# Two attention layers on one core: the order of GpSimd's first work, and the clock that orders the instructions

## The chip, the cores and the metric

The kernel runs on one core of a Trainium2 chip. The metric is the device time of the whole program in microseconds (us). A core has a matrix engine (TensorE, PE in the profile, with its weight loads as PEld), three engines for elementwise work (VectorE or DVE, ScalarE or ACT, GpSimd or POOL), and SyncE (SP), which here only issues transfers. Transfers between memory and the core are issued by SP, ACT and POOL, each through a queue of its own, and moved by 16 DMA engines. Each engine works through its own list of instructions in the order in which the program wrote them, and waits on semaphores where it needs another engine's result.

## The reference

Two attention layers of the same size (2048 positions, width 1024, 32 heads of 32) on different inputs; their outputs stand side by side.

```python
def _A_ref(x, wqkv, wo):          # W, dil = 8, 2: each position sees itself and 7 earlier ones, every second one
    q, k, v = heads(x @ wqkv)
    logits = einsum("bhsd,bhswd->bhsw", q, k[gathered]) * scale      # masked with -1e9
    o = einsum("bhsw,bhswd->bhsd", softmax(logits), v[gathered])
    return merge(o) @ wo
def _B_ref(x, wqkv, wo):          # W = 256: each position sees itself and the 255 before it
    scores = where(mask, einsum("bhqd,bhkd->bhqk", q, k) * Dh ** -0.5, -1e9)
    o = einsum("bhqk,bhkd->bhqd", softmax(scores), v)
    return merge(o) @ wo
return concatenate([a, b], axis=-1)
```

## The kernel before, in words

**Units.** The work is cut into eight units of 512 positions: four of layer B ("dense"), then four of layer A ("dilated"; even and odd positions are separated on the host, so that a window of stride two becomes one of stride one). In each unit there are eight head groups of four heads, so 64 groups in all.

**Numbers in two parts.** Every fp32 operand of a projection is split into a high part (a rounded copy, `fp32r`) and a low part (operand minus high part); three products of parts replace one fp32 product. The split of a loaded tile is done in `Stream.parts`: a cast on ACT (L249) or DVE (L252), then one subtraction on DVE for each 512 columns (L255). So each loaded weight tile of 1024 columns costs a cast and two subtractions in a row.

**Loads.** `Stream` has one list of items (x tiles and weights) in the order of use, 512 KB each. The first six go out at once from SP and ACT, in halves where `FIRST` says so. All later ones go out from POOL (L194) into three rotating buffers; a load can start when the splits of the item three before it have read its buffer. `load_to(n)` issues loads until `n` items are loaded, and `split_to(n)` splits items and books, for the end of each split, the next call of `load_to`. The first call, at L163, asks for six items (`NRAW + len(more)`).

**Attention, dense layer.** For a group, q and k are evacuated from PSUM, split (L597, L601), and copied by SP into stacked buffers `qst` and `kst` (L621, L552 for the 256 keys of the unit before). There are two of each, used in turn. Then come 16 first scores (`s`, 96 partitions), for each of which DVE adds the mask and takes the maximum (L1356) and ACT takes the exponential and its sum (L1361); from these one row of logarithms is formed and multiplied into the stack (L1396). The second scores follow, already normalised, ACT takes the exponential into `pbuf` (L1441), and `keep` (L1417) zeroes what lies outside the window, by an affine_select on POOL (L1420) or a minimum with a mask on DVE (L1423). Two P·V matmul groups per head group follow ("o" on TensorE), each after the masks of its blocks.

**Attention, dilated layer.** Each group is copied into a seat (L580), 64 small score blocks are computed in one go, DVE runs a softmax over them (L1184 to L1214), ACT spreads the result (L1223, L1226), and P·V follows. The last eight keys of a unit are kept in `tails` for the next one (L565 reads them, L570 writes them, L568 clears them on DVE where the next unit begins a new sequence: eight times in unit 5).

**Constants.** `constants` (L452) makes masks and the identity on POOL with memsets and affine_selects (L463 to L483).

**The order.** Nothing is reordered by a compiler: the kernel is written in the order of a small simulation. `Clock` keeps a time at which each engine is free (`free`), and the main loop (L1576) takes, of four lists (auxiliary, second scores with P·V, first scores, gemm), the item that can start first by that clock; ties go to the lists in this order. An item starts on TensorE as soon as the clock thinks that what it needs is ready. `use` books an instruction on an engine, `issue` and `move` book a transfer and return when it lands, `defer` puts off work to a time of the clock, `flush` runs what is due. A choice between two engines (`parts`, `keep`, `copy_out`) compares the ends by the clock; `keep` takes POOL if it ends no more than 0.2 after DVE (`MASK_BIAS`). First scores of a dense group are held back 1.2 (`KEYS_LATE`) after the stacked copies land by the clock.

**How the clock treats shared things before the change.** POOL and a DVE instruction with two SBUF operands (`port=True`) exclude one another: POOL starts after the last such DVE instruction that has been booked, and DVE after the last POOL instruction booked. All transfers stand in one row: each takes a duration in which nothing else moves, in the first gap that holds it, and lands a tail later. `MOVE` has both numbers by kind; `LEAD` is the time from issue to the start (SP 1.34).

**The first call of `load_to`.** The loop over `FIRST` at L171 uses the name `n` for its counter, which is the name of the function's argument. After the loop `n` is 8, and the function goes on to issue items 6 and 7 from POOL, before `constants` is reached, which is run as the main loop begins. The same counter is tested against `BY_ACT` at L174.

## Time and profile before

| | us |
|---|---|
| median of 3 runs | 1803.32 |
| lowest, highest | 1802.33, 1803.51 |
| the profiled execution | 1802.41 |
| its span, first to last instruction | 1800.7 |
| mean granted TensorE clock | 0.999 |

The profile shows one execution. Its parts: busy time of each engine, the span in 40 slices, the DMA queues, the chain of work that ended last, the costliest groups of instructions, and the DMA issues. A row of the timeline has the start, the time until the end of the merged instructions, engine, line, operation, output and inputs, count, and in brackets the idle time before it with what ended it. A row of waits has who waited for whom, the total, the number of times, and the longest. A row of a group has the number of instructions, then busy time and the mean of one in ns, then idle time before them. Everything on TensorE is issued by one helper, so all its rows have the line L297, and are told apart by tiles: g for projections, s for scores, o for P·V. The chain that ended last is 87% PE:

```
PE 87%; DVE 5%; issue 3%; DMA 2%; ACT 2%; POOL 1%; DVEq 0%; POOLq 0%; ACTq 0%
```

### The profile page before, as it was taken

Reading aid. Unit: us, or ns where it says so; the run is one execution under the profiler, and the core shown is the slowest. Engines: PE = TensorE matmul, PEld = TensorE weight load, DVE = VectorE, ACT = ScalarE, POOL = GpSimd, SP = SyncE. Lnnn points to the kernel's source line nnn. Section 1 sums busy time; section 2 is a strip of 40 time slices with the busy share of each in tenths; the row PEclk is TensorE's granted clock in tenths of the full one; section 3 lists DMA queues with packets and bytes.
Section 4 is the critical chain, followed back from the end, with each engine's and each line's share of the span. In section 5 each row is a group of like instructions: output and inputs, shape, how many; then the busy total and the mean of one; then the engine's idle time right before and its main releaser. Section 6 shows DMA issues by size and latency. Waiting matters only on the chain.

```text
span 1800.7 us, 38453 instructions
## 1 busy us (share of the span) xinstructions
PE 1775.3 (99%) x14496; PEld 1439.2 (80%) x14496; DVE 1297.4 (72%) x2887; ACT 940.3 (52%) x2336; POOL 413.7 (23%) x952
## 2 busy tenths in 40 slices
PE   9999999999999999999999999999999999999999
PEld 7787777888777888778788778877888787778887
DVE  6777876768867769867678566756666768688866
ACT  4565566555656565655655444534454435355442
POOL 3222323222242222332223400110011101001120
PEclk9999999999999999999999999999999999999999
DMA  8354664644645555455546265665466558758984
GB/s 245 112 152 135 185 167 135 171 138 138 185 141 172 152 131 167 144 159 148 141 124 174 84 190 180 213 211 187 160 212 204 192 177 285 265 181 273 350 287 146
DMA packets 154794, 324.58 MB, mean 180 GB/s; under 512 B 18032, under 2 KB 58992, under 8 KB 154608
## 3 DMA queue, kind: packets, MB, share of 16 engines
q0 software_dynamic: 45792, 166.74, 29.8%
q1 hardware_dynamic: 98736, 137.02, 26.6%
q10 hardware_dynamic: 10080, 18.35, 2.7%
q8 instruction: 115, 1.88, 0.4%
q14 instruction: 71, 0.58, 0.1%
HBM read 201.33 MB, written 53.48 MB: 142 GB/s over the span
## 4 chain that ended last, share of the span: by engine, by line
PE 87%; DVE 5%; issue 3%; DMA 2%; ACT 2%; POOL 1%; DVEq 0%; POOLq 0%; ACTq 0%
PE g L297 68%; PE s L297 13%; PE o L297 6%; DMA raw<-xs 1%; DVE w L255 1%; DVE x L255 1%; ACT s L1361 0%; DVE band L1212 0%; DMA raw<-wv 0%; DVE sm L1208 0%; DVE band L1184 0%; ACT w L249 0%; DMA raw<-wqk 0%; DVE w L252 0%; DMA qst<-nat 0%
## 5 line engine op out<-in xcount | busy, mean ns | idle before, releaser
L297 PE MATMUL g<-x,w 128*128 128x512 f32 x3552 | 878.9, 393 | 5.0 <-DVE x L255 3.9
L297 PEld LDWEIGHTS g<-x,w 128*128 128x128 f32 x3552 | 654.8, 188 | 135.2 <-issue 6.6
L255 DVE TENSOR_TENSOR w<-raw,w 128x512 fp32r<-128x512 f32 x510 | 334.3, 697 | 48.5 <-ACT w L249 42.4
L1361 ACT ACTIVATE s<-s,nm 128x384 f32<-128x384 f32 (+2 forms) x512 | 274.4, 537 | 108.2 <-DVE nm L1356 101.7
L1356 DVE CUSTOM_DVE_ANT_0 s<-s,mask_d 128x384 f32<-128x384 f32 (+2 forms) x512 | 261.7, 553 | 91.7 <-PE s L297 91.4
L297 PE MATMUL g<-w,x 128*128 128x256 f32 (+1 forms) x1728 | 307.9, 327 | 2.4 <-DVE w L255 1.5
L1420 POOL TENSOR_SCALAR_AFFINE_SELECT pbuf<-pbuf 128x128 f32<-128x128 f32 (+1 forms) x603 | 218.4, 390 | 317.9 <-ACT pbuf L1441 315.9
L297 PEld LDWEIGHTS g<-w,x 128*128 128x128 f32 x1728 | 255.2, 190 | 28.0 <-DVE w L255 2.8
L297 PE MATMUL g<-r,w 128*128 128x512 f32 x960 | 239.0, 393 | 1.7 <-issue 1.2
L1441 ACT ACTIVATE pbuf<-s 128x384 f32<-128x384 f32 (+2 forms) x480 | 203.1, 505 | 64.2 <-PE s L297 62.0
L297 PEld LDWEIGHTS g<-r,w 128*128 128x128 f32 x960 | 177.2, 188 | 37.2 <-issue 2.0
L194 POOL DMA_DIRECT2D raw<-wqk x126 | 68.6, 544 | 407.4 <-DVE w L255 256.8
L297 PEld LDWEIGHTS s<-qst,kst 128*128 128x128 f32 x704 | 113.4, 188 | 42.6 <-ACT s L1361 16.8
L297 PE MATMUL s<-kst,qst 96*128 96x384 f32 (+2 forms) x512 | 142.6, 342 | 0.9 <-ACT s L1361 0.7
L297 PE MATMUL s<-qst,kst 128*128 128x256 f32 (+2 forms) x704 | 137.0, 302 | 4.0 <-ACT s L1361 3.2
L252 DVE CAST w<-raw 128x1024 fp32r<-128x1024 f32 x173 | 119.8, 692 | 19.3 <-PE g L297 9.0
L249 ACT CAST w<-raw 128x1024 fp32r<-128x1024 f32 (+1 forms) x83 | 85.8, 1038 | 71.1 <-PE g L297 29.7
L297 PEld LDWEIGHTS s<-kst,qst 96*128 96x128 f32 x512 | 93.6, 189 | 26.3 <-issue 4.4
L1361 ACT ACTIVATION_READ_ACCUMULATOR s<-s,nm 128x1 f32 x512 | 105.3, 206 | 0.0
L1223 ACT COPY wide<-band 32x512 f32<-32x512 f32 x128 | 79.0, 617 | 31.0 <-DVE band L1214 29.4
L297 PE MATMUL o<-pbuf,vbuf 128*32 128x384 f32 (+2 forms) x1408 | 91.2, 388 | 0.0
L597 ACT ACTIVATE nat<-g 128x512 fp32r<-128x512 f32 x64 | 38.3, 598 | 98.2 <-PE g L297 89.0
(90 smaller groups left out, 1432.1 us busy)
## 6 DMA issues: line engine op xcount, KB each, us to landing
raw<-wqk POOLq DMA_DIRECT2D x126, 512.0 KB, 4.6
raw<-wv POOLq DMA_DIRECT2D x60, 512.0 KB, 5.0
qst<-nat SPq DMA_DIRECT2D x96, 256.0 KB, 5.7
kst<-nat SPq DMA_DIRECT2D x96, 256.0 KB, 5.7
raw<-wo POOLq DMA_DIRECT2D x44, 512.0 KB, 4.4
raw<-xs POOLq DMA_DIRECT2D x28, 512.0 KB, 4.5
outs<-ost ACTq DMA_DIRECT2D x38, 256.0 KB, 3.1
kst<-halo SPq DMA_DIRECT2D x72, 128.0 KB, 4.5
```

The costliest lines, as they stand in the source:

```text
L194: (self.nc.scalar if early else self.nc.gpsimd).dma_start(raw if len(ap.shape) == 2 else raw.rearrange("p (a b) -> p a b", a=2), ap)
L249: nc.scalar.copy(t[:, 0, :], raw)
L252: nc.vector.tensor_copy(t[:, 0, :], raw)
L255: nc.vector.tensor_tensor(t[:, 1, c:c + 512], raw[:, c:c + 512], t[:, 0, c:c + 512].bitcast(F32), op=ALU.subtract)
L297: nc.tensor.matmul(out, left, right, **k)
L597: nc.scalar.activation(hl[:, 0, :], ps, AF.Copy, scale=sc)
L1223: nc.scalar.copy(diag[r:r + 32, :, :, c:c + 32], turned[r:r + 32, :, :, 1, :])
L1356: nc.vector.tensor_tensor_reduce(ps[:, :n], ps[:, :n], mask[:, cut:full], scale=-1.0, scalar=BIG, op0=ALU.add, op1=ALU.min, accum_out=nm)
L1361: nc.scalar.activation(ps[:, :n], ps[:, :n], AF.Exp, bias=nm, scale=-1.0, accum_out=sm)
L1420: nc.gpsimd.affine_select(w, w, pattern=[[0, m], [step, n]], compare_op=ALU.is_ge, fill=0.0, base=base, channel_multiplier=chan)
L1441: nc.scalar.activation(w, ps[:, :pack * n].rearrange("p (j n) -> p j n", j=pack), AF.Exp)
```

## The change

Four edits, in one file.

1. The counter of the loop over `FIRST` is renamed `turn`. The first call of `load_to` then ends with six items; items 6 and 7 are loaded when their buffers' splits end by the clock, which is after `constants`.
2. The clock's load is shorter with a longer tail, the sum being the same. `move` now books SP's and ACT's transfers in one row and POOL's in another; a new transfer waits for the last one of its row, and goes at half speed while one of the other row is under way. What is booked is not lengthened afterwards.
3. POOL's start in the clock is held only by the DVE instruction (with two SBUF operands) in whose booked time it falls, until that one's end. DVE still waits for the last POOL instruction booked.
4. The clearing of `tails` goes from DVE to GpSimd.

```diff
-    MOVE = dict(load=(2.12, 0.14), store=(0.64, 0.4), copy=(1.18, 0.56),
+    MOVE = dict(load=(1.5, 0.76), store=(0.64, 0.4), copy=(1.18, 0.56),
...
-        self.port = dict(dve=0.0, pool=0.0)
-        self.later, self.lands, self.busy = [], [], []
+        self.port, self.held = 0.0, []
+        self.later, self.lands, self.moves = [], [], [[], []]
...
         if eng == "pool":
-            t = max(t + 0.06, self.port["dve"])
-        elif port:
-            t = max(t, self.port["pool"])
-        return t
+            t += 0.06
+            return next((e for s, e in self.held if s <= t < e), t)
+        return max(t, self.port) if port else t
...
-        if eng == "pool" or port:
-            self.port[eng] = end
+        if eng == "pool":
+            self.port = end
+        elif port:
+            self.held = [x for x in self.held if x[1] > self.now - 5.0] + [(end - dur, end)]
...
-        return self.move(start + self.LEAD[eng], *self.MOVE[kind])
+        return self.move(eng, start + self.LEAD[eng], *self.MOVE[kind])
...
-    def move(self, t, dur, tail):
-
-        busy = self.busy = [x for x in self.busy if x[1] > self.now - 20.0]
-        i = 0
-        while i < len(busy):
-            if busy[i][1] <= t or busy[i][0] < t:
-                t = max(t, busy[i][1])
-            elif busy[i][0] - t >= dur:
+    def move(self, eng, t, dur, tail):
+
+        mine, other = self.moves[eng == "pool"], self.moves[eng != "pool"]
+        t = begin = max(t, mine[-1][1] if mine else 0.0)
+        for s, e in other:
+            if e <= t:
+                continue
+            n = max(s - t, 0.0)
+            if n >= dur:
                 break
-            else:
-                t = busy[i][1]
-            i += 1
-        busy.insert(i, (t, t + dur))
+            t, dur = t + n, dur - n
+            n = min((e - t) / 2, dur)
+            t, dur = t + 2 * n, dur - n
+            if not dur:
+                break
+        mine.append((begin, t + dur))
+        del mine[:-40]
         return t + dur + tail
...
-            for n, (i, h) in enumerate(FIRST):
+            for turn, (i, h) in enumerate(FIRST):
...
-                queue, took = (self.nc.scalar, self.ck.load) if n in BY_ACT else (self.nc.sync, self.ck.copy)
+                queue, took = (self.nc.scalar, self.ck.load) if turn in BY_ACT else (self.nc.sync, self.ck.copy)
...
-                    ck.defer(e + 1.0, lambda: (nc.vector.memset(tails[:, s, :], 0.0), ck.use("dve", 0.08, ck.now)))
+                    ck.defer(e + 1.0, lambda: (nc.gpsimd.memset(tails[:, s, :], 0.0), ck.use("pool", 0.08, ck.now)))
```

## The prediction

> **What bounds the kernel now.** I read the page's totals first, then the busy time of each engine in three stretches (start, dense layer, dilated layer), then who TensorE waited for in each.

> ```profile
> span 1800.7 us, 38453 instructions
> PE 1775.3 (99%) x14496; PEld 1439.2 (80%) x14496; DVE 1297.4 (72%) x2887; ACT 940.3 (52%) x2336; POOL 413.7 (23%) x952
> 0.00:40.00 40.00, 36.50 (x148) 28.34 (x149) 22.72 (x49) 18.43 (x32) 16.86 (x35) 1.00 0.79 234
> 40.00:1040.00 1000.00, 993.45 (x6052) 801.62 (x6051) 746.40 (x1923) 579.27 (x1684) 305.56 (x755) 1.00 0.53 149
> 1040.00:1800.00 760.00, 745.38 (x8300) 609.23 (x8298) 528.29 (x919) 342.57 (x621) 91.28 (x163) 1.00 0.67 219
> ```

> The columns of the last three rows are length, then busy time of PE, PEld, DVE, ACT, POOL, the granted clock, the DMA share and GB/s. TensorE works 1775.3 of 1800.7 us, and the diff touches no matmul. So an order can only give or take TensorE's waits: 3.5 us in the start (40.00 - 36.50), 6.6 in the dense layer, 14.6 in the dilated layer, some of them not movable (first loads, tail). Who ended them, in us, times, longest; first the start, then the dense, then the dilated stretch:

> ```profile
> PE s L297 <- DVE qst L1569: 1.5, 1, 1.5
> PE g L297 <- DVE w L252: 0.6, 1, 0.6
> ...
> PE s L297 <- ACT s L1361: 4.6, 7, 1.0
> PE s L297 <- DVE hl L1382: 0.6, 2, 0.3
> PE s L297 <- DVE qst L1396: 0.6, 2, 0.4
> ...
> PE g L297 <- DVE x L255: 3.6, 2, 2.8
> PE s L297 <- issue: 2.2, 1, 2.2
> PE g L297 <- DVE w L255: 2.2, 5, 0.8
> ```

> No row names a DMA: transfers reach TensorE only through the engine that splits them. Most movable waits end on VectorE or right behind it (ACT's exponential at L1361 needs VectorE's maximum). That is where a gain can be, and it is about 0.8% at the very most, 14 us.

> **The change part by part.**

> *Constants and loads at the start.* Items 6 and 7, the first two loads on GpSimd's queue, now come behind the constants.

> ```profile
> 5.46 0.69 DVE L255 TENSOR_TENSOR x<-raw,x 128x512 fp32r<-128x512 f32 x1 [3.99 <-ACT x L249]
> 6.07 0.68 DVE L255 TENSOR_TENSOR w<-raw,w 128x512 fp32r<-128x512 f32 x1
> 7.70 1.90 DVE L255 TENSOR_TENSOR x<-raw,x 128x512 fp32r<-128x512 f32 x3 [0.95 <-ACT x L249]
> 8.70 0.68 POOL L194 DMA_DIRECT2D raw<-wqk  x1 [8.19 <-DVE x L255]
> 9.91 0.55 POOL L194 DMA_DIRECT2D raw<-wqk  x1 [0.53 <-DVE x L255]
> 10.45 0.22 POOL L463 MEMSET keep_d<- 128x128 f32 x1
> 10.74 3.83 POOL L464 TENSOR_SCALAR_AFFINE_SELECT ident<-keep_d 128x128 fp32r<-128x128 f32 x1
> 12.52 1.29 DVE L255 TENSOR_TENSOR r<-pbuf,r 128x512 fp32r<-128x512 f32 x2
> 13.73 0.69 DVE L252 CAST w<-raw 128x1024 fp32r<-128x1024 f32 x1
> 14.69 1.11 POOL L469 TENSOR_SCALAR_AFFINE_SELECT pick<-pick 32x16 f32<-32x16 f32 x2
> 17.59 3.38 POOL L477 TENSOR_SCALAR_AFFINE_SELECT near<-near 32x200 f32<-32x200 f32 x8
> 19.69 2.88 PE L297 MATMUL g<-x,w 128*128 128x512 f32 x12
> 22.39 0.51 POOL L457 TENSOR_SCALAR_AFFINE_SELECT keep_d<-keep_d 128x128 f32<-128x128 f32 x1
> 22.93 2.19 POOL L194 DMA_DIRECT2D raw<-wv  x3
> 30.55 0.69 DVE L252 CAST w<-raw 128x1024 fp32r<-128x1024 f32 x1 [7.10 <-DMA raw<-wv]
> 31.30 0.50 PE L297 MATMUL g<-w,x 128*128 128x512 f32 x1 [0.56 <-DVE w L252]
> 32.63 0.72 PE L297 MATMUL g<-w,x 128*128 128x512 f32 x2 [0.83 <-DVE w L255]
> ```

> The constants ran from 10.45 to 22.90, 12.45 us. Of that, some 4.5 were waits for VectorE: 3.83 for ident where the median affine_select takes 0.293 (row below), 1.11 for two tiny ones, a little in the last. Undisturbed they take about 8 us. Nothing holds them now, so they start near 0.5, when VectorE is idle, and would end at 8.5. But VectorE works from 5.46 to 6.75, and from 7.70 to 13.8 back to back (to 14.4 with item 6's cast). About 4.9 + 0.95 us are free for GpSimd before 7.70, so 2 us are left over, and the ident row says what becomes of such a rest: it stays until the run ends, here at 13.7, since the cast at 13.73 is of item 6, which has not come. Then the load of item 6 leaves near 15.4 instead of 8.70, lands 4.6 later (below) at 20.0, and is cast at 20.7. TensorE wanted it at 19.69 and its third product needs a subtraction more: **+1.3**. Bounds: 0, if the rest slips through (a load by 13 is in time), and +2.3, if the rest runs until 16.2. For the first subtractions VectorE can meet a GpSimd operation under way, up to 3.38 / 8 = 0.4 us each: +0.2. On the other side the three loads at 22.93 (wv) leave as soon as their buffers are free, the first right behind item 7 near 17, and the two waits of TensorE at 31.30 and 32.63 go, 0.56 + 0.83: **-1.4**. Start in sum +0.1, between -1.4 and +1.3. What is late next would be item 7, wanted two rows of 2.88 later, near 25.4, landing near 21: covered.

> *GpSimd's masks.* The clock no longer holds GpSimd until the last booked VectorE subtraction, only until the one it falls into. So `keep` (which gives GpSimd a preference of 0.2) finds GpSimd earlier. Masks in the dense layer, VectorE's and GpSimd's, with the least, median and largest duration in ns:

> ```profile
> L1423 DVE TENSOR_TENSOR pbuf<-pbuf,keep_d x71: 277/294/619, 59.5 to 1017.1; 128x128 f32<-128x128 f32 x43, 128x256 f32<-128x256 f32 x28
> L1423 DVE TENSOR_TENSOR pbuf<-pbuf,keep_f x62: 277/373/611, 59.7 to 1017.3; 128x128 f32<-128x128 f32 x37, 128x256 f32<-128x256 f32 x25
> L1420 POOL TENSOR_SCALAR_AFFINE_SELECT pbuf<-pbuf x603: 282/293/920, 55.8 to 1028.4; 128x128 f32<-128x128 f32 x109, 128x256 f32<-128x256 f32 x42
> PEld o L297 <- POOL pbuf L1420: 1.3, 4, 0.4
> ```

> How many of VectorE's 71 + 62 = 133 (some 44 us, by the medians) move, the trace cannot say: between none and all. I take two thirds, as the old rule overstated GpSimd's start and the new one rather understates it. That takes 29 of VectorE's 746 us away, in the stage where 4.6 + 0.6 + 0.6 = 5.8 us of TensorE's waits hang on VectorE. In proportion: **-3.9** (0 to -5.8). GpSimd has room (305.56 of 1000). The price is a mask that ends later than the clock thinks, with the P·V group behind it on TensorE: 1.3 us now; I take **+0.5** more, and bound it by the first rival.

> *Transfers.* A load alone lands when it did (2.12 + 0.14 = 1.50 + 0.76), but beside a copy the two now share, instead of standing in one row.

> ```profile
> raw<-wqk POOLq DMA_DIRECT2D x126, 512.0 KB, 4.6
> qst<-nat SPq DMA_DIRECT2D x96, 256.0 KB, 5.7
> 1521.95 1.88 PE L297 MATMUL g<-x,w 128*128 128x512 f32 x7 [2.78 <-DVE x L255]
> ```

> A copy that begins with a load was thought to land 2.12 + 1.18 + 0.56 = 3.86 us later. It is now 0.75 done when the load ends at 1.50, and lands at 1.50 + 0.43 + 0.56 = 2.49, 1.4 earlier. Scores and splits are put earlier by up to that. Work on TensorE hides it in the dense layer, as gemm items fill whatever an attention item leaves. Where gemm items themselves run short, near 1521, a split behind a softmax on VectorE costs 2.78. An order that splits earlier saves it, one that splits later adds another; it is the nearest row for both signs. I take **-1.0**, as loads are now expected earlier, between -3.6 and +3.6 (the stage's whole wait on DVE x, won or had once more).

> *The tails memset*, eight times, VectorE to GpSimd.

> ```profile
> L568 DVE MEMSET tails<- x8: 65/65/65, 1173.0 to 1326.5; 128x8 f32 x8
> DVE tails L568 <- ACT nat L565: 10.9, 4, 4.8
> ```

> Its 0.5 us are nothing, but in four of eight VectorE stood for 10.9 us in all at ACT's L565, with splits queued behind it. GpSimd takes over that wait, and queued behind it there are weight loads, which are issued two or three items ahead (24 matmuls each, twice the 2.88 of the row at 19.69). One load late by 4.8 us at the worst is covered by that. VectorE's gain is worth something only where TensorE waits for splits, 2.2 us in five places of the layer: **-0.6** (-2.2 to +0.6).

> **Sum.** 0.1 - 3.9 + 0.5 - 1.0 - 0.6 = -4.9. The profiled execution took 1802.41 (span 1800.7), so 1797.5. It stands 0.9 below the median of the runs shown, 1803.32 (1802.33 to 1803.51); against the median: **1798.4**, or 0.27% faster.

> **Rivals.**

> ```profile
> L255 DVE TENSOR_TENSOR w<-raw,w 128x512 fp32r<-128x512 f32 x510 | 334.3, 697 | 48.5 <-ACT w L249 42.4
> ```

> *Masks that come too late (slower).* Place: the 64 P·V groups of the dense layer (two for each of 32 head groups). VectorE's subtractions come in pairs, and the new clock lets a mask go after the first of a pair; the ident row shows GpSimd standing through a whole run. A group whose last mask meets that is late by one subtraction, 0.697. The pairs fill about a fifth of VectorE's time (334.3 of 1800.7), so their first halves meet a tenth of the groups, and a fifth if two masks count in each; with a sixth, 64 / 6 x 0.697 = +7.4. Without the dense gain: 1802.4 + 0.1 + 7.4 - 1.6 = 1808.3, median 1809. It outweighs the gain of 4.9 from seven late groups on. For it: GpSimd items start when predicted, with no margin. Against: only 4 waits of 1.3 us in 603 masks so far.

> [...]

> *Keys that come too late (slower).* The copies take 5.7 from issue to landing, against 1.34 + 1.18 + 0.56 = 3.08 in the clock when alone: 2.6 more. The old clock added up to 2.12 beside a load and has a margin of 1.2 (`KEYS_LATE`); the new one adds 0.75 and the margin, 0.65 short. At a DMA share of 0.53 that meets 17 of 32 groups: +11, so 1802.4 + 0.1 - 3.9 + 0.5 - 0.6 + 11 = 1809.5, median 1810. Against: part of the 5.7 is the copy ahead in its own queue, which both clocks book; and the buffers are double, so that many copies are early.

> *Waits that only move.* TensorE has other work nearly everywhere, the start cancels out, and what VectorE gains in one place goes elsewhere: 1803, give or take 3.6. For it: 99% busy.

> **Chances.** Forecast, with all larger gains: 0.45. Waits that only move: 0.23. Late masks 0.18, late keys 0.14. What a measurement of this kernel tells from no change is about 0.2%, 3.6 us: below 1799.7 is faster, 0.45; above 1806.9 slower, 0.32; between 0.23. The forecast's own range is 1791 (the dense and transfer terms at their better ends: 1803.3 + 0.1 - 5.8 - 3.6 - 2.2 is 1791.8) to 1800. The range for 8 in 10 reaches to the late masks: 1791 to 1809.

> **What would show it.** Right: constants on GpSimd ending before 10 or standing until 14 to 16; item 6 loaded after them; no wait at 31 to 33; fewer than 70 masks on VectorE, TensorE's wait for ACT s at L1361 down from 4.6 to about 1; no wait of VectorE for L565. Wrong: TensorE waiting for pbuf at L1420 for more than 5 us, or at the first score of a group for the copies; a longer wait than 2.78 in the dilated layer; a stall above 2 us near 20.

## The result, and the profile after

The changed kernel takes **1816.78 us** (median of 6 runs, 1811.79 to 1818.09), the kernel before, beside it, 1803.41 (6 runs): **1.0062 times as long, 95% interval 1.0048 to 1.0077**. The forecast was 1798.4, and the time lies outside the range of 1791 to 1809. The profiled execution took 1816.79, its span is 1815.1, 14.4 more than before; the mean granted clock is 0.996 (0.999 before).

The totals of the page of after, and its busy time in the same three stretches, with the columns as before:

```profile
PE 1786.0 (98%) x14496; PEld 1442.8 (79%) x14496; DVE 1303.6 (72%) x2898; ACT 937.1 (52%) x2325; POOL 418.1 (23%) x952
...
PE 83%; DMA 6%; DVE 5%; ACT 2%; issue 2%; POOL 1%; SPq 0%; ACTq 0%; DVEq 0%; POOLq 0%
```

```profile
0.00:40.00 40.00, 38.19 (x158) 30.39 (x159) 25.82 (x58) 21.32 (x43) 13.53 (x35) 1.00 0.88 267
40.00:1040.00 1000.00, 987.78 (x5992) 792.68 (x5991) 742.19 (x1918) 572.71 (x1664) 310.81 (x743) 1.00 0.52 147
1040.00:1815.00 775.00, 760.01 (x8349) 619.70 (x8347) 535.58 (x923) 343.09 (x620) 93.75 (x174) 1.00 0.67 216
```

TensorE has the same 14496 matmuls and is idle for 29.1 us (1815.1 - 1786.0) instead of 25.4, so only 3.7 us of the loss is idle time in the profile's sense. The other 10.7 are in its busy time (1786.0 against 1775.3). Two things are counted in it: pieces at half clock (13.65 us in the clock record of after, 3.41 in that of before), and, by estimate, waits too short to be told as idle. In the chain that ended last, transfers have 6% instead of 2%. The start gained: in 40 us TensorE did 38.19 us of work instead of 36.50. The dense stretch lost: 12.2 us without work (1000 - 987.78) instead of 6.6.

**Start.** The timeline of after, GpSimd's first and last constants and its first loads, and one row of TensorE:

```profile
0.81 0.20 POOL L468 MEMSET keep_d<- 128x128 f32 x1 [0.29 <-POOLq L1644]
1.08 0.29 POOL L469 TENSOR_SCALAR_AFFINE_SELECT ident<-keep_d 128x128 fp32r<-128x128 f32 x1
3.72 4.04 POOL L482 TENSOR_SCALAR_AFFINE_SELECT near<-near 32x200 f32<-32x200 f32 x8
9.34 0.47 POOL L462 TENSOR_SCALAR_AFFINE_SELECT keep_d<-keep_d 128x128 f32<-128x128 f32 x1
9.95 1.23 POOL L199 DMA_DIRECT2D raw<-wqk  x2
19.63 2.88 PE L302 MATMUL g<-x,w 128*128 128x512 f32 x12
30.98 1.55 PE L302 MATMUL g<-w,x 128*128 128x512 f32 x6
```

The constants run from 0.81 to 9.81, and items 6 and 7 leave one behind the other from 9.95 on, where before they left at 8.70 and 9.91. TensorE starts its row at 19.63 without a wait; the waits of before at 31.30 and 32.63 are gone.

**Who TensorE waited for.** The waits of after, in the dense and then the dilated stretch, and what VectorE waited for among the transfers:

```profile
PE s L302 <- ACT s L1366: 8.8, 10, 1.8
...
PE g L302 <- DVE band L879: 3.9, 2, 3.1
```

```profile
DVE x L257 <- DMA raw<-xs: 12.1, 6, 4.0
DVE r L1110 <- DMA r<-od: 10.2, 4, 3.7
```

First scores wait 8.8 us instead of 4.6 for a bank of PSUM that ACT's exponential frees (L1366, L1361 before). That is the part that the waits show. The weight loads of the same matmuls wait too, and this is the clearest difference of the two traces. The groups of TensorE's weight loads, before and then after (number, busy time and mean in ns, idle time before them and what ended it):

```profile
L297 PEld LDWEIGHTS s<-kst,qst 96*128 96x128 f32 x512 | 93.6, 189 | 26.3 <-issue 4.4 <-ACT s L1361 2.7 <-ACT pbuf L1441 1.1
```

```profile
L302 PEld LDWEIGHTS s<-kst,qst 96*128 96x128 f32 x512 | 93.8, 190 | 39.2 <-ACT s L1366 19.3
```

2.7 us became 19.3. VectorE, which had waited 3.0 us at most for any one kind of transfer after 40 us, now waits 12.1 for the x tiles of the next unit.

**What one such place looks like.** The timeline of after where the x tiles of a dense unit arrive:

```profile
436.40 0.55 POOL L199 DMA_DIRECT2D raw<-xs  x1
436.96 2.77 POOL L1425 TENSOR_SCALAR_AFFINE_SELECT pbuf<-pbuf 128x128 f32<-128x128 f32 x6
439.68 1.07 POOL L199 DMA_DIRECT2D raw<-xs  x2
448.40 0.43 DVE L257 CAST x<-raw 128x512 fp32r<-128x512 f32 x1 [3.56 <-DMA raw<-xs]
451.14 0.56 DVE L1361 CUSTOM_DVE_ANT_0 s<-s,mask_d 128x384 f32<-128x384 f32 x1
452.52 1.01 PE L302 MATMUL s<-kst,qst 96*128 96x384 f32 x2 [1.31 <-ACT s L1366]
```

GpSimd has six masks in front of two loads, which then leave back to back. The cast of one stands at the head of VectorE's list for 3.56 us, the maxima (L1361 is now the line of VectorE's mask and maximum) stand behind it, ACT's exponential behind those, and TensorE at the end of the row waits for the bank. The price in idle time is 1.31.

**The half clock.** It costs more than 1.31, as the windows of after around two such places show (before had one piece of this kind, near 1435):

```profile
440.00:460.00 20.00, 18.19 (x115) 15.04 (x115) 15.07 (x44) 9.54 (x30) 2.72 (x5) 0.91 0.77 221
...
1680.00:1700.00 20.00, 19.90 (x109) 15.95 (x110) 16.81 (x27) 8.48 (x12) 3.70 (x7) 0.85 0.95 336
```

A granted clock of 0.91 over 20 us is half speed for about 3.4 us (20 x 0.09 x 2 = 3.6), so a loss of at most 1.7 us that counts as busy time. 0.85 is twice that, some 3. The clock record in the trace of after has three such pieces, of 3.41, 3.41 and 6.83 us, 13.65 in all, against one of 3.41 in before. So half clock accounts for at most 5.1 of the 10.7 us by which busy time grew, (13.65 - 3.41) / 2; the rest would be waits too short to be told as idle.

**Where the loss builds up.** For each kernel I added up its matmuls, each weighed with the time that one of its shape takes in an undisturbed row (0.2275 us for g 128x512, 0.176 for a first score of 384, and so on), and compared the times at which the kernels have done equal work. Another choice of these times per shape moves an entry by up to some 1.5 us, so small entries mean little. "At" is before's time, the others are us against it; the right columns belong to experiments below.

| at | after | e1_start | g1_banks_later | h3_before_banks |
|---|---|---|---|---|
| 74 | -2.3 | -1.6 | -3.0 | -2.4 |
| 275 | -0.5 | -1.5 | -1.9 | -1.6 |
| 532 | +3.7 | -1.7 | -2.2 | +3.2 |
| 789 | +7.5 | -1.8 | -0.5 | +12.2 |
| 981 | +12.2 | -1.7 | -0.5 | +12.6 |
| 1471 | +6.5 | -0.8 | -0.9 | +16.5 |
| 1655 | +5.9 | -0.4 | -0.6 | +17.8 |
| end | +14.4 | -0.6 | +9.0 | +17.6 |

After is ahead by 2.3 us, loses it and 12 more in the dense layer, makes half of that good, and loses 8.5 in some 60 us near the end.

### The profile page after: what moved, and what is told of

Its sections match the earlier page's. It is cut to its first block, busy times and chain, and to the rows that moved or that the text cites. A ratio compares the mean times of both kernels' runs of the same rounds, so it can differ in the third digit from the quotient of the medians.

```text
span 1815.1 us, 38436 instructions
## 1 busy us (share of the span) xinstructions
PE 1786.0 (98%) x14496; PEld 1442.8 (79%) x14496; DVE 1303.6 (72%) x2898; ACT 937.1 (52%) x2325; POOL 418.1 (23%) x952
## 3 DMA queue, kind: packets, MB, share of 16 engines
q8 instruction: 115, 1.88, 0.4%
## 4 chain that ended last, share of the span: by engine, by line
PE 83%; DMA 6%; DVE 5%; ACT 2%; issue 2%; POOL 1%; SPq 0%; ACTq 0%; DVEq 0%; POOLq 0%
PE g L302 65%; PE s L302 12%; PE o L302 6%; DMA raw<-xs 3%; DVE w L260 1%; DMA od<-r 1%; DMA r<-od 1%; ACT s L1366 1%; DVE x L260 1%; POOL pbuf L1425 1%; DVE s L1361 1%; DMA outs<-band 0%; DMA raw<-tv 0%; DVE qst L1401 0%; ACT w L254 0%
## 5 line engine op out<-in xcount | busy, mean ns | idle before, releaser
L1361 DVE CUSTOM_DVE_ANT_0 s<-s,mask_d 128x384 f32<-128x384 f32 (+2 forms) x512 | 261.9, 555 | 125.6 <-PE s L302 124.4
L1366 ACT ACTIVATE s<-s,nm 128x384 f32<-128x384 f32 (+2 forms) x512 | 273.7, 535 | 125.8 <-DVE nm L1361 125.5
L1425 POOL TENSOR_SCALAR_AFFINE_SELECT pbuf<-pbuf 128x128 f32<-128x128 f32 (+1 forms) x595 | 226.2, 409 | 276.1 <-ACT pbuf L1446 274.3
L302 PE MATMUL s<-kst,qst 96*128 96x384 f32 (+2 forms) x512 | 148.8, 347 | 9.6 <-ACT s L1366 8.0
L302 PEld LDWEIGHTS s<-qst,kst 128*128 128x128 f32 x704 | 109.5, 189 | 39.3 <-ACT s L1366 20.5
L302 PEld LDWEIGHTS s<-kst,qst 96*128 96x128 f32 x512 | 93.8, 190 | 39.2 <-ACT s L1366 19.3
L1366 ACT ACTIVATION_READ_ACCUMULATOR s<-s,nm 128x1 f32 x512 | 104.6, 204 | 0.0
L199 POOL DMA_DIRECT2D raw<-wv x60 | 38.7, 645 | 245.1 <-DVE w L260 134.8
L1228 ACT COPY wide<-band 32x512 f32<-32x512 f32 x128 | 79.0, 617 | 19.8 <-DVE band L1219 17.6
## 6 DMA issues: line engine op xcount, KB each, us to landing
raw<-wqk POOLq DMA_DIRECT2D x126, 512.0 KB, 4.1
raw<-wv POOLq DMA_DIRECT2D x60, 512.0 KB, 4.1
qst<-nat SPq DMA_DIRECT2D x96, 256.0 KB, 4.3
kst<-nat SPq DMA_DIRECT2D x96, 256.0 KB, 4.0
raw<-wo POOLq DMA_DIRECT2D x44, 512.0 KB, 4.6
raw<-xs POOLq DMA_DIRECT2D x28, 512.0 KB, 5.9
outs<-ost ACTq DMA_DIRECT2D x38, 256.0 KB, 2.1
```

The lines of the kernel that those rows point to most:

```text
L199: (self.nc.scalar if early else self.nc.gpsimd).dma_start(raw if len(ap.shape) == 2 else raw.rearrange("p (a b) -> p a b", a=2), ap)
L302: nc.tensor.matmul(out, left, right, **k)
L1228: nc.scalar.copy(diag[r:r + 32, :, :, c:c + 32], turned[r:r + 32, :, :, 1, :])
L1361: nc.vector.tensor_tensor_reduce(ps[:, :n], ps[:, :n], mask[:, cut:full], scale=-1.0, scalar=BIG, op0=ALU.add, op1=ALU.min, accum_out=nm)
L1366: nc.scalar.activation(ps[:, :n], ps[:, :n], AF.Exp, bias=nm, scale=-1.0, accum_out=sm)
L1425: nc.gpsimd.affine_select(w, w, pattern=[[0, m], [step, n]], compare_op=ALU.is_ge, fill=0.0, base=base, channel_multiplier=chan)
```

## The experiments

Ratios are to the kernel before, run beside each on the same chip. Each answer has its 95% interval.

**One part alone.** `e1_start` renames the counter and does nothing else. `e2_transfers` has the new `MOVE` and `move` alone, `e3_port` the new rule for GpSimd alone (third edit), `e4_all_but_transfers` is the changed kernel with the old `MOVE` and `move`.

```diff
# e1_start, against before
-            for n, (i, h) in enumerate(FIRST):
+            for turn, (i, h) in enumerate(FIRST):
# e3_port, against before
-            t = max(t + 0.06, self.port["dve"])
+            t += 0.06
+            return next((e for s, e in self.held if s <= t < e), t)
```

> The kernel before with the renamed loop counter alone: constants ahead of the loads of items 6 and 7, all else as it was. Theory (the start is a gain of its own: constants end near 9.8, no waits of TensorE at 31 to 33): 1800 to 1802, 1.4 to 2.4 us less than before, granted clock as before. Rival (whatever moves the order costs several us): 1806 or more.

> The kernel before with the new transfer booking alone (load 1.50 + 0.76 and the two rows at half speed). Theory (transfers are now booked to land too early, so VectorE stands at splits and sums whose data has not come): 1810 to 1817, VectorE's waits for DMA (x at its cast, r at its sums) up from 2.3 to 15 us or more, one or more added stretches of half clock. Rival (the port rule is what costs): 1801 to 1805.

> The kernel before with the new rule for GpSimd's start alone. Theory (transfers are the cause): 1800 to 1806, VectorE's waits for DMA within 3 us of those of before. Rival (masks or the new mask order cost the time): 1808 to 1817, and VectorE waits for DMA no longer than before, TensorE's wait for ACT s up.

> The changed kernel with the old transfer booking put back (so start, port rule and tails are new). Theory (transfers cost 10 us or more, the start gains 2): 1798 to 1804, VectorE's waits for DMA below 5 us. Rival (port rule): 1808 to 1816. Rival (any new order costs, whichever part makes it): 1806 to 1812.

| | us | ratio |
|---|---|---|
| e1_start | 1802.07 | 0.9990 (0.9979 to 1.0000) |
| e2_transfers | 1824.97 | 1.0125 (1.0107 to 1.0143) |
| e3_port | 1819.88 | 1.0096 (1.0078 to 1.0113) |
| e4_all_but_transfers | 1818.76 | 1.0085 (1.0071 to 1.0098) |

The start is 1.6 us better and stays so until 981; then a stall that the profile puts down to issue brings a half-clock piece (timeline of e1_start):

```profile
1055.44 0.28 PE L297 MATMUL s<-pbuf 32*32 32x40 f32 x9 [1.62 <-issue]
1055.64 4.61 PE L297 MATMUL g<-x,w 128*128 128x512 f32 x12
```

Twelve matmuls take 4.61 us here, 2.88 in the row at 19.63. Each of the two rules alone costs more than the whole change: 1.25% and 0.96% of 1803.4 us, 22.5 + 17.3 = 40 us in sum, against 11.2 (0.62%) for all four edits. So the parts don't add, and what each is worth can't be read from its absence either: without the transfers the change is not better (0.85%). The weight loads of first scores wait for ACT s 16.0 us in e2_transfers, 15.4 in e3_port and 15.7 in e4_all_but_transfers: either rule brings the same wait. Half of the second edit brings some of it (10.4 in e5_number, 11.1 in e6_rows, both below). VectorE's wait for raw<-xs, 12.1 in after, is there with the rule for GpSimd (11.5 in e3_port, 11.6 in e4_all_but_transfers) and hardly with the transfers (2.6 in e2_transfers). So banks are waited for just as long where the x tiles are not late, and late x tiles are not needed for it.

**Neutral changes.** Does any other order cost this much? Three numbers of the clock were set off by a hundredth of a us or so in the kernel before, with no meaning behind it.

```diff
# n1_neutral_act
-    SEEN = dict(act=0.15, dve=0.115, pool=0.08)
+    SEEN = dict(act=0.16, dve=0.115, pool=0.08)
# n2_neutral_copy
-    ... copy=(1.18, 0.56),
+    ... copy=(1.18, 0.61),
# n3_dve
-    SEEN = dict(act=0.15, dve=0.115, pool=0.08)
+    SEEN = dict(act=0.15, dve=0.11, pool=0.08)
```

> The kernel before with one number of the clock moved by 10 ns (the delay after which ScalarE's result is seen, 0.15 to 0.16), which says nothing truer or less true of the chip, but changes the order from the first units on (1977 lines of difference on TensorE). Theory (the new booking and the port rule are worse descriptions): 1800 to 1806, as before. Rival (the order of before is the one good one that was found, and any other order costs): 1808 to 1822, with waits of VectorE for DMA x and added stretches of half clock.

> The kernel before with copies booked to land 50 ns later (tail 0.56 to 0.61), a smaller change of order (382 lines on TensorE). Theory (descriptions matter): 1800 to 1806. Rival (any other order costs): 1806 to 1820.

> The kernel before with one number of the clock set off by 5 ns (the delay with which others see VectorE's results, 0.115 to 0.110 us). It has no meaning of its own and changes the order of TensorE from some 15% of its rows on. Theory that a reorder alone costs: 1806 to 1815, with half-clock pieces and waits for ACT s above those of before (4.6 us). Rival, that only the two new rules cost: 1801 to 1805.

Measured: n1_neutral_act 1812.34 us, 1.0042 (1.0022 to 1.0063). n2_neutral_copy, which moves little, 1804.64, 1.0005 (0.9992 to 1.0018). n3_dve 1811.57, 1.0039 (1.0023 to 1.0055). Two of the three reorders for no reason cost 0.4%, the smallest one nothing. By the working of the table above n1 and n3 lose it in the dense layer, some 11 and 8 us by 981, about as much as after. The wait of after is weaker in them: at the weight loads of first scores ACT s has 3.1 us in n1, 3.0 in n2 and 6.9 in n3 (2.7 in before, 19.3 in after), and issue comes first there with 3.9 to 7.4. n1 and n3 lose at other places, first of all TensorE's wait for VectorE's row of logarithms, 0.6 us in before. It is 3.0 in n3_dve; the waits of n1_neutral_act in the dense stretch:

```profile
PE s L297 <- ACT s L1361: 5.3, 8, 1.0
PE s L297 <- DVE hl L1382: 4.1, 2, 2.1
```

**Two remedies that failed.** If the x tiles that come late were the cause, an order that expects them later should lose less; if the sums of the last stage were (VectorE's wait for r<-od), likewise.

```diff
# f1_x_later, against after
-(self.ck.load if early else self.ck.fetch)("load", self.ck.now)
+(...)("load", self.ck.now) + (3.0 if self.items[self.loaded][0] == "x" else 0.0)
# f2_sums_later, against after
-BG_REST, BG_SLACK, BG_EARLY = 2.0, 1.5, 8.0
+BG_REST, BG_SLACK, BG_EARLY = 2.0, 5.0, 12.0
```

> The changed kernel with x tiles booked to land 3.0 us later by the clock, so that VectorE's x casts stand later in its list. Theory (the dense layer's loss is VectorE standing at x casts whose load shares its time with other transfers): VectorE's wait for DMA raw<-xs from 12.1 to below 3, TensorE's wait for ACT s from 8.8 to below 5, no half clock at 447 and 713, 1805 to 1810. Rival (something else in those stretches): 1812 to 1818, though the wait for xs is gone.

> The changed kernel with the background sums booked 3.5 and 4.0 us later (1.5 to 5.0 and 8.0 to 12.0), which leaves the dense layer as it is. Theory (the loss of 11 us at 1655 to 1690 begins with VectorE's sums standing at the transfer r<-od, 10.2 us in four waits): those waits below 3, no half clock near 1672, 1804 to 1809. Rival (the end is bound by the stores and the band, whatever the sums do): 1813 to 1818.

f1_x_later 1826.47, 1.0127 (1.0104 to 1.0149), and VectorE's wait for raw<-xs stayed (12.4), so this edit did not do what it was meant to and does not test the theory. f2_sums_later 1815.32, 1.0067 (1.0041 to 1.0093): the wait for r<-od fell from 10.2 to 0.3, and the time did not change. In its place TensorE waits in the dilated layer for other things:

```profile
PE g L302 <- DVE w L260: 3.9, 6, 1.9
PE g L302 <- issue: 3.6, 1, 3.6
```

**A margin for banks.** `BANK_LATE` is the time after which the clock, once it has a bank free, lets scores take it. Set to 0.3 in the changed kernel; the same in the kernel before (with the two small edits, counter and tails, which stand alone in `e8_start_tails`).

```diff
# g1_banks_later (against after), h3_before_banks (against e8_start_tails)
-BANK_LATE = 0.0
+BANK_LATE = 0.3
```

> The changed kernel with one margin set up: first scores, rows and second scores are taken 0.3 us after the clock has their bank free (0.0 so far). Theory (the new order asks for banks that ACT's exponential has not freed yet; this is the largest term of the 13 us): the wait of TensorE for ACT s in the dense layer falls from 8.8 to below 5 us, and the time from 1816.8 to 1805 to 1811. Rival (the lost time is made of stalls of all kinds that any large reorder throws up, and only changes place): the wait for ACT s falls, but the time stays between 1812 and 1820.

> The kernel before with the two small edits alone: the renamed counter and the clearing of tails on GpSimd; the clock's transfers and its rule for GpSimd stay. Theory (the two new rules of the clock lose the time, through an order for which this kernel's margins were not set; the start gains 1.6 to 2.4 us, and the tails cost nothing that lasts): 1799 to 1802 us, ratio 0.997 to 1.000, TensorE's waits for ACT s in the dense layer at most 6 us. Rival (any change of the order, however small, loses 0.4% or more): 1808 or more.

> The kernel before with the renamed counter and the clearing of tails on GpSimd, and banks taken 0.3 us later. Theory (before had room enough by its old rules, so that a margin gains nothing): 1802 to 1810, wait of TensorE for ACT s 1 to 4 us. Rival (the margin is good for any order): below 1800.

| | us | ratio |
|---|---|---|
| g1_banks_later | 1812.29 | 1.0050 (1.0034 to 1.0066) |
| e8_start_tails | 1803.59 | 0.9996 (0.9985 to 1.0006) |
| h3_before_banks | 1817.66 | 1.0071 (1.0055 to 1.0086) |

In g1_banks_later the wait is gone, as the waits in its dense stretch and its weight loads show:

```profile
PE s L302 <- ACT pbuf L1446: 2.4, 4, 0.6
...
PE s L302 <- ACT s L1366: 1.2, 2, 1.0
```

```profile
L302 PEld LDWEIGHTS s<-kst,qst 96*128 96x128 f32 x512 | 92.1, 189 | 23.3 <-ACT s L1366 5.0 <-issue 3.8
```

With it went the whole loss up to 1655 (table above: -0.6 instead of +5.9, and -0.5 instead of +12.2 at 981). VectorE's wait for raw<-xs fell from 12.1 to 0.4 too, and this run alone doesn't say which of the two is the cause; e2_transfers, with 16.0 us for the banks and 2.6 for the x tiles, speaks against the x tiles. By its time the run is still the rival's (1812 to 1820), because of the end. In the order of before, the same margin does the opposite: +12 by 789, weight loads waiting 11.2 us for ACT s, 1.0071. It is no repair in itself, but one more number that suits one order and not another.

**The end.** g1_banks_later still loses 9.6 us in its last stage. Its timeline there:

```profile
1659.12 2.87 DVE L1110 TENSOR_TENSOR r<-r 128x512 f32<-128x512 f32 x4 [4.22 <-DMA r<-od]
1661.91 0.68 DVE L879 TENSOR_TENSOR ost<-g,r 128x512 f32<-128x512 f32 x1
1662.64 3.02 PE L302 MATMUL g<-x,w 128*128 128x512 f32 x12 [1.38 <-DVE ost L879]
1676.18 0.69 DVE L879 TENSOR_TENSOR band<-g,r 128x512 f32<-128x512 f32 x1 [2.87 <-DMA outs<-band]
1677.01 5.27 PE L302 MATMUL g<-x,w 128*128 128x512 f32 x15 [3.91 <-DVE band L879]
```

Sums stand on VectorE for a transfer, the evacuation at L879 (L874 before) behind them, TensorE behind that. h1_banks_sums gives both margins.

```diff
# h1_banks_sums, against after
-BANK_LATE = 0.0
+BANK_LATE = 0.3
-BG_REST, BG_SLACK, BG_EARLY = 2.0, 1.5, 8.0
+BG_REST, BG_SLACK, BG_EARLY = 2.0, 5.0, 8.0
```

> The changed kernel with two margins set up: banks 0.3 us (as in the run that took 0.5% more than before and had lost nothing until 1650 us), and the sums of the last stage 5.0 instead of 1.5 us after their loads by the clock. Theory (the new rules need larger margins, and the loss sits in these two places): the end no longer waits for band and the time is 1800 to 1805, as before. Rival (a stall of the end goes elsewhere, as when the sums alone were later): 1809 to 1814, with TensorE losing some 10 us between 1640 and 1720 again.

1811.45 us, 1.0040 (1.0028 to 1.0052): the rival. TensorE no longer waits for band, but for splits of weights (dilated stretch of h1_banks_sums):

```profile
PE g L302 <- DVE w L260: 7.7, 6, 3.3
```

What matmuls took beyond their undisturbed time between 1640 and 1730 is 4.5 us in before, 16.3 in after, 14.7 in g1, 14.0 in h1, 16.3 in f2 and 15.9 in e4. The causes change (band 3.9, 5.6, 0, 0, 0.6 from after to e4; half clock about 2.9, 1.6, 3.1, 5.1, 2.8), and the sum hardly does. But this stage does not cost every order. The same 90 us of before, h3_before_banks, e3_port and after, with the columns as in the stretches above:

```profile
1640.00:1730.00 90.00, 89.72 (x585) 73.19 (x584) 76.30 (x123) 47.21 (x77) 18.77 (x33) 1.00 0.97 345
1640.00:1730.00 90.00, 89.86 (x773) 72.50 (x773) 78.67 (x129) 44.85 (x76) 17.42 (x30) 1.00 0.90 312
1640.00:1730.00 90.00, 83.79 (x703) 67.03 (x703) 70.81 (x115) 46.02 (x76) 16.86 (x29) 0.98 0.88 297
1640.00:1730.00 90.00, 83.51 (x574) 66.53 (x573) 71.70 (x116) 42.40 (x69) 17.87 (x31) 0.96 0.92 318
```

TensorE is idle here for 0.1 to 1.0 us, at full clock, in all seven orders made by the old rules (before, e1, e8, n1, n2, n3, h3), and for 4.9 to 7.6 us, at a granted clock of 0.94 to 0.98, in all eleven that have the second edit, one half of it (e5_number and e6_rows, below), or the third. n1, n3 and h3, which lose 0.4 to 0.7% elsewhere, lose nothing here. So the loss of the last stage goes with the new rules and not with any reorder; by what step they bring it about stays open.

**Are landings booked too early?** h2_late_landings puts 0.9 us on every load, copy and store in the clock; e5_number and e6_rows split the second edit.

```diff
# h2_late_landings, against after
-    MOVE = dict(load=(1.5, 0.76), store=(0.64, 0.4), copy=(1.18, 0.56),
+    MOVE = dict(load=(1.5, 1.66), store=(0.64, 1.3), copy=(1.18, 1.46),
# e5_number, against before (e6_rows: before's numbers with the new move)
-    MOVE = dict(load=(2.12, 0.14), store=(0.64, 0.4), copy=(1.18, 0.56),
+    MOVE = dict(load=(1.5, 0.76), store=(0.64, 0.4), copy=(1.18, 0.56),
```

> The changed kernel with 0.9 us more on the tail of each load, copy and store in the clock (0.76, 0.56 and 0.40 become 1.66, 1.46 and 1.30), since on the chip a load takes 4.6 us and a copy 4 to 5.7 from issue to landing and the clock has 3.7 and 3.1. Theory that the new clock lands transfers too early and that this costs: 1802 to 1809, VectorE's waits for raw<-xs and r<-od (12.1 and 10.2 us) below 4 each. Rival, that transfers are not the cause but VectorE's and ACT's work behind each other: waits for transfers fall, the wait of TensorE for ACT s stays near 8.8 us, and the time between 1812 and 1820.

> The kernel before with the load's numbers of the clock alone (1.50 and 0.76 for 2.12 and 0.14), all transfers in one row as before. Two rows alone cost 39 us, both halves of the edit 21. If the halves add, this gains 18: below 1790. Theory (each reorder brings its own stalls, and the halves do not add): 1805 to 1820.

> The kernel before with two rows of transfers in the clock (shared at half speed), but the old numbers for a load (2.12 and 0.14). Theory that the booking in two rows is what costs (loads and copies thought to land earlier than in one row): 1815 to 1825, as with both halves of the edit (1825). Rival, the shorter load of 1.50 with its tail of 0.76 costs: 1800 to 1808 here.

h2_late_landings 1822.9 us, 1.0107 (1.0092 to 1.0122): no repair, with raw<-xs at 12.8. e5_number 1823.13, 1.0110 (1.0094 to 1.0126); e6_rows 1843.44, 1.0213 (1.0188 to 1.0238), with a granted clock of 0.988. Two rows cost 2.1%, the shorter load 1.1%, both together 1.25%: again no sum.

Eight of the sixteen runs (e2, e3, e4, e5, e6, f1, h2, h3) came out slower than every range given for them: the price of a new order was put too low again and again.

## Why the prediction was wrong

*The start (+0.1, between -1.4 and +1.3).* Mechanism half right, size wrong: the gain is 1.6 us (e1_start) to 2.3 (after at 74), a little past the better bound. (By its own terms the worse bound was 2.3 + 0.2 - 1.4 = +1.1, not +1.3.) The waits at 31 to 33 went as said. The +1.3 for a late item 6 did not come: I had GpSimd stand until 13.7, as ident had, but the constants from 7.83 to 9.81 ran while VectorE did four subtractions (7.65 to 10.35), and none took more than 0.58. Eight selects for near took 4.04 us instead of 3.38. In the profiled run of e1_start the gain was spent again by one half-clock piece; 0.9990 reaches from -0.2% to nothing.

*The masks (-3.9).* **This step failed first.** Two thirds of VectorE's 133 masks were to move. The masks of after on VectorE and GpSimd (least, median, largest in ns):

```profile
L1428 DVE TENSOR_TENSOR pbuf<-pbuf,keep_d x77: 276/291/1009, 59.7 to 1001.2; 128x128 f32<-128x128 f32 x67, 128x256 f32<-128x256 f32 x10
L1428 DVE TENSOR_TENSOR pbuf<-pbuf,keep_f x64: 277/285/565, 59.9 to 1001.5; 128x128 f32<-128x128 f32 x50, 128x256 f32<-128x256 f32 x14
L1425 POOL TENSOR_SCALAR_AFFINE_SELECT pbuf<-pbuf x595: 282/331/952, 54.6 to 1028.8; 128x128 f32<-128x128 f32 x131, 128x256 f32<-128x256 f32 x68
```

77 + 64 = 141 are on VectorE, eight more than before, and e3_port, which has the rule for GpSimd alone, has 77 + 65 = 142. So the rule does not move masks to GpSimd in this kernel. It was read by itself, as if the order around it stood still; that masks come at other times in the new order is the likely reason, not a shown one. The conversion was unfounded too: 29 of VectorE's 746 us are 4% of its work, and the sum took two thirds of TensorE's 5.8 us of waits for them. The wait for ACT s, which was to fall from 4.6 to about 1, rose to 8.8.

*Late masks (+0.5, and the rival at 1809).* Not it: 1.6 us against 1.3 in before, in five places (waits of after).

```profile
PEld o L302 <- POOL pbuf L1425: 1.6, 5, 0.4
```

No P·V group paid more than 0.4 us. The median mask went from 293 to 331 ns because more masks are wide (200 of 128x256 instead of 171); by shape the medians stayed, 292 ns for the narrow ones and 406 or 407 for the wide ones, and only the mean of the narrow ones rose, from 347 to 372.

*Late keys (rival at 1810).* Not it either. The copies land earlier than before (issues of after, KB and median us from issue to landing; 5.7 both before), and TensorE has no wait for them:

```profile
qst<-nat SPq DMA_DIRECT2D x96, 256.0 KB, 4.3
kst<-nat SPq DMA_DIRECT2D x96, 256.0 KB, 4.0
...
raw<-xs POOLq DMA_DIRECT2D x28, 512.0 KB, 5.9
```

The transfers that became later are the loads of x, 5.9 against 4.5. What stands behind them is VectorE's own list (12.1 us of waits).

*The transfers (-1.0, bounds -3.6 and +3.6).* The bounds were the failure in size: this edit alone costs 1.25%, some 22.5 us, six times the upper bound, and the rule for GpSimd alone 0.96%, 17.3 us, where I had a gain of 3.4. I had priced the edit by the one wait it seemed to touch, near 1521. It changes the clock for every transfer, and with that the order of the instructions.

*The tails (-0.6).* VectorE's 10.9 us of waits for L565 went to GpSimd, as said (waits of after):

```profile
POOL tails L573 <- ACT nat L570: 26.5, 7, 11.8
```

They grew to 26.5, and one lasts 11.8 and not 4.8. ScalarE's wait for x tiles grew there too (13.7 us between 1160 and 1345, 8.8 before), but TensorE waits only 0.7 us in that stretch, against 2.4 in before, so it cost nothing. e8_start_tails with the memset moved (0.9996) can't be told from e1_start without (0.9990).

*The premise and the whole.* The prediction began with "an order can only give or take TensorE's waits", and that failed: with the same 14496 matmuls TensorE's busy time grew by 10.7 us, its idle time by 3.7. "Waits that only move" came nearest to the mechanism, but it let gains and losses cancel. They don't, and this is the deeper step that was missing: the sum took a new order to be the old one with a few places changed. n1 and n3 show that another order of this kernel can lose 0.4% by itself, and h3 that a number such as `BANK_LATE` which helps one order can cost another 0.7%.

In the last stage the new rules have a loss of their own beside this, as far as these eighteen orders tell (some 8 of after's 14.4 us are lost there). In the dense layer it is not settled. For it: the wait for ACT s that marks after is there with either rule alone (15.4 to 16.0 us), much weaker in the three neutral runs (3.0 to 6.9), and in g1 it goes together with the loss of the dense layer. Against it: n1 and n3 lose about as much there, and h3, with the old rules and one margin changed, has 11.2 us of that wait.

One reason would fit but was not tried by itself: the kernel's own clock, read after its last instruction (no measurement, a number of the program), stands at 1836.4 for before, later than the chip's 1800.7, and at 1794.2 for after, earlier than the chip's 1815.1. An order that expects everything later than it comes would have slack in every wait, and the new rules would have taken it out. In the seven orders by the old rules it stands 21 to 36 us later than the chip, in the eleven others at most 4 us later and mostly earlier, the same division as in the last stage. h2_late_landings is no test of this: its clock stands at 1795.1, nearly where after's does. n1, at 1833.1, loses in the dense layer without this, so it is not the whole.

No version here beats the kernel before by more than the measurement tells: e1_start is the best with 0.9990 (0.9979 to 1.0000).

## What to carry to other kernels

Where one clock orders a whole kernel, an edit to the clock is a new order, and its price is not the sum of the places that it seems to touch: before trusting a gain of a few us, change a number of the clock by nothing that matters and see how far the time moves (here up to 0.4%). A clock that agrees better with single durations need not order better; margins found with the old one belong to it, and have to be found again. When a wait is taken away and the time stays, look for what comes due next in the same stretch before taking away another.

## What the hardware showed that was not expected

**Half clock.** The clock record of after has TensorE at half speed for pieces of 3.41, 3.41 and 6.83 us. The second begins at 720.12, 0.31 us after the end of a wait of 0.93; the wait of 0.75 at 712 was followed by none (timeline of after):

```profile
712.61 1.00 PE L302 MATMUL s<-kst,qst 96*128 96x384 f32 x2 [0.75 <-ACT s L1366]
719.81 1.25 PE L302 MATMUL s<-kst,qst 96*128 96x384 f32 x2 [0.93 <-ACT s L1366]
720.85 2.76 PE L302 MATMUL g<-x,w 128*128 128x512 f32 x6
```

```profile
1057.76 0.28 PE L297 MATMUL s<-pbuf 32*32 32x40 f32 x9 [2.17 <-issue]
```

**GpSimd beside VectorE.** Alone, in before, VectorE's first two subtractions took 0.69 and 0.68 us; with the eight selects of near running on GpSimd beside them, 0.80 and 0.84 (timeline of after):

```profile
5.52 0.80 DVE L260 TENSOR_TENSOR x<-raw,x 128x512 fp32r<-128x512 f32 x1 [4.05 <-ACT x L254]
6.25 0.84 DVE L260 TENSOR_TENSOR w<-raw,w 128x512 fp32r<-128x512 f32 x1
```

VectorE's two took 0.11 and 0.16 us longer, and the eight selects 0.66 (4.04 against 3.38), where in before one select, ident, took 3.83 (0.29 in after).
